# Wider spacing of the cosine chains, goals per period for the weight conversion, and earlier y rows in a fused attention and two-layer feed-forward kernel

## The chip, the cores and the metric

The kernel runs on one core of one Trainium2 chip. The metric is the device time of one execution in microseconds. PE is TensorE's matrix engine, PEld its weight loads, DVE is VectorE, ACT is ScalarE, POOL is GpSimd, and SP is SyncE, which here issues nearly all DMAs.

## The reference, cut to what matters

```python
def reference(q, k, v, omega, moe_*, moe2_*):
    q_p, k_p = phi(q * scale), phi(k * scale)      # random features: exp of a projection
    x = (q_p @ (k_p.T @ v)) / (q_p @ k_p.sum(0) + 1e-06)     # per head; 4 x 8 heads, 576 rows
    x = x.transpose(0, 2, 1, 3).reshape(2304, 512)
    xn = x / sqrt(mean(x * x) + 1e-06) * rms_g
    x = (silu(xn @ w_gate) * (xn @ w_val)) @ w_out          # layer 1: 512 -> 1536 -> 512
    h = x @ moe2_w_in                                       # layer 2: 512 -> 2048 -> 512
    return (h * cos(h)) @ moe2_w_out
```

The large weights of both layers arrive as float64, that is as pairs of 32-bit words; the kernel computes in float32.

## The kernel before

Every matrix product of the two layers is made of three passes over float32 values that are split into a high and a low part, so a weight has to be turned into such a pair before PE can use it. Class `Weights` does this in two halves. A **front** takes one chunk (128x512) from two 32-bit words to one float32: ACT scales the exponent (L182), DVE works on the bits (L190, L193 for some chunks, L195, L204) and POOL adds the low part (L209); the result is stored to DRAM (`keep`, L347). A **back** fetches it again, on every second chunk makes sums and differences on DVE (L274, L287, L289, L291), and splits it (ACT L214, POOL L217) into a buffer of a ring of 20. Neither has a place of its own: `pace(front, back)` adds two rates to two credits and runs as many steps as the credits allow, so these steps go into each engine's queue wherever `pace` is called. `rate(chunks, steps)` says how many front steps a call must run for `chunks` chunks to be done after `steps` calls. A back whose chunk isn't kept yet, or that finds no free buffer, is put off.

The program has four stages: attention (to 96 us), layer 1's first part (96 to 301 us), where attention's last rows, four columns of hidden units and the weights share a step, layer 1's second and third part (301 to 590 us) and layer 2. From 301 us on the products are made in pairs of blocks with seven multiplications in place of eight (functions `duo`, `ys`, `hidden`).

Layer 2 runs in 24 **periods** (k = 0 to 23). A period has seven products `hidden(k, i)`, i = 0 to 6, each of six matmuls into one of two PSUM banks, Xh or Yh, by turns. A product adds to what the bank's last one left, so PE can't begin product i + 2 before the bank has been read for product i: for i = 0, 2, 3, 6 by an ACT copy (L1190), for i = 1, 4, 5 by a DVE addition (L1193). Twice in a period, after products 1 and 5, `cosine` starts a **chain** on two rows of features: ACT counts the turns (Identity), DVE takes them off (two operations, `reduce`), ACT takes the sine, DVE multiplies (L1225), ACT and DVE split the result (`cut`, L1046 and L1049). Between the products PE gets `share[i]` matmuls of the output products `out2` (36 to a period, L1242), which run about a period behind because they need the chains' results. `out2` ends a run of periods on the same blocks in periods 4, 7, 13, 16, 21 and 23 (`ends_run` two periods before): its six sums are then taken out of PSUM by `evict` (L1267, L1274, L1276), and the next run begins in the same banks.

What comes when is told by a clock of **units**: `at(d, f)` puts `f` off by d units, and `unit()` runs what is due, then `pace(*tempo)`, which is the front and back rate of the period. There are two units to a product, so 14 to a period. Each engine then works its queue strictly in the order in which the code issued it.

`ask` (in `after_second`) fetches a y row from DRAM `later` units after a product; `add_y` (L1099) adds it to layer 1's sum; `mix` makes from the sums the combinations that layer 2 reads.

Of the kernel before, what the change touches and what calls it, by code (L numbers as in the profile page):

```python
# [38 lines left out]
AF = mybir.ActivationFunctionType  # L39
ALU = mybir.AluOpType  # L40
# [16 lines left out]
def attention_then_ffn(ctx: ExitStack, tc: tile.TileContext, qT, kT, v, omT, wc1, rms_g, wc2, out, B, H, S, D):  # L57
    nc = tc.nc
# [486 lines left out]
    with tc.manual_schedule():  # L545
# [402 lines left out]
        for n, (g, blk, f, first, last) in enumerate(steps):  # L948
            tail = n >= N1 - G
            if tail:  # L950
                wts.freed = C1 * f
            back = 2.0 if tail else wts.rate_back(C1 * G + 5, N1 - G - n) / 2
            if wts.n_front < 6 * FRONT:
                back = 0.0
            rates = wts.rate(FRONTS_BY_1, N1 - G + 1 - n) / 2 if n <= N1 - G else 0.0, back
            if n < G:
                rates = max(rates[0], 4), rates[1]
            s = SLOTS + 2 * n
            load_ahead(s)
            older(s, -7, -5)  # L960
            ps = product(blk, f, 0)
            a = silu(blk, f, ps)
            older(s, -6, -4, -3, -2, -1)
            begin(s)
            if n >= 1:
                out1(*steps[n - 1][:3], hid[n - 1], *steps[n - 1][3:], (0, 1))
            older(s, 1, 0)
            job(2 if tail else 3)
            wts.pace(*rates)
            job(0 if tail else 3)  # L970
            if n > N1 - G and early_names:
                bring(1, 0, early_names.pop(0))
            flush(3)
            load_ahead(s + 1)
            older(s + 1, -7, -5)
            ps = product(blk, f, 1)
            hid[n] = gated(blk, f, a, ps)
            older(s + 1, -6, -4, -3, -2, -1)
            begin(s + 1)
            if n >= 1:  # L980
                out1(*steps[n - 1][:3], hid.pop(n - 1), *steps[n - 1][3:], (2, 3))
            older(s + 1, 1, 0)
            job(2 if tail else 3)
            wts.pace(*rates)
            job(0 if tail else 3)
            flush(3)
            if n == N1 - G:
                assert s + 2 > max(then)
                while len(combined) < 2:
                    job(1)  # L990
                combine.close()
                open_between()
                limit[0] = NPAIR
                tp[:] = [combine.enter_context(tc.tile_pool(name="combinations2", bufs=3, reuse_waits="tile")), 3]
                early_names = ["B11", "B21", "T2", "T1", "T4"]
            if n >= N1 - G and early_names:
                bring(1, 0, early_names.pop(0))
# [206 lines left out]
        def cosine(k, h, of, begin=1):  # L1204

            name = "_".join(f"{x}_{f}_{blk}" for x, f, blk in of)
            span = slice(0, 2) if len(of) == 2 else slice(begin, begin + 1)
            h = h[:, span]
            a = two_rows(I32, f"turns{name}")[:, span]
            b = f32(halves(f"r{name}"))[:, span]  # L1210
            r = f32(a)

            def reduce():
                nc.vector.scalar_tensor_tensor(b, a, -TWO_PI_HI, h, op0=ALU.mult, op1=ALU.add)  # L1214
                nc.vector.scalar_tensor_tensor(r, a, -TWO_PI_LO, b, op0=ALU.mult, op1=ALU.add)  # L1215

            def cut(i):
                o = turned[of[i]] = halves("o%d_%d_%d" % of[i])
                split(o, r[:, i])
                at(int(of[i][0] + 1 < NPER), lower, o, r[:, i], nc.vector)  # L1220

            at(1, nc.scalar.activation, a, h, AF.Identity, quarter, 1.0 / (2 * math.pi))
            at(2, reduce)
            at(3, nc.scalar.activation, r, r, AF.Sin, half_pi)
            at(4, lambda: nc.vector.tensor_tensor(r, h, r, op=ALU.mult))  # L1225
            for i in range(len(of)):
                at(5 + i, cut, i)

        def out2(k):

# [57 lines left out]
        for k, (g, p) in enumerate(pairs):  # L1288
# [10 lines left out]
                made["y"] = 0  # L1299
            front[0] = wts.rate(FRONTS_BY_2, left) if left > 0 else 0.0  # L1300
            tt = {}
            later = 3 if g == 1 else 9

            def after_first(i, f):
                if k == 0 and i == 0 and f == fs[1]:
# [25 lines left out]
                wts.freed = start + PER_GROUP  # L1331
            if g == 2:
                for m, (name, kk) in enumerate((name, kk) for kk in range(2) for name in ("T1", "T3", "T2", "T4")):
                    at(6 + 3 * m // 2 if p else 6 + (0, 2, 3, 6)[m % 4] + 14 * kk, mix, p, name, kk)

        def stream():
            for k in range(NPER):
# [2 lines left out]
        def freed_by(k):  # L1340
# [4 lines left out]
            elif sessions[n - 1][0] != g and fq == GROUPS2[g][0]:  # L1345
                wts.freed = first_tile[g]

        o = stream()
        for k in range(1, NPER):
            loading = ends_run[k]  # L1350
            tempo[:] = 0.0 if loading or k < 4 else wts.rate(len(wts.todo) + 1, 14 * (14 - k)), 0.5 if loading else 1.3
            if ends_run[k - 1]:
                ask_sums(k - 1)
            share = [2, 3, 3, 4, 4, 5, 5] if k == 1 else [5, 5, 3, 5, 6, 6, 6] if begins_run[k - 1] else [5, 5, 5, 5, 5, 5, 6]
            for i in range(7):
                if (k, i) == (len(GROUPS2[0]), 4):
                    assert not whole
# [5 lines left out]
                for _ in range(share[i]):  # L1363
                    next(o)
                unit()
                if i == 1 and k > 1:
                    freed_by(k - 1)
                if (i, k + 1) == (3, NPER):
                    ask_sums(k)
# [53 lines left out]
```

## Time and profile before

| what | us |
|---|---|
| time, median of 3 (from, to) | 992.25 (991.57, 992.88) |
| profiled execution: time | 990.3 |
| profiled execution: span | 988.5 |
| PE busy (share of the span) | 957.0 (97%) |
| DVE busy | 730.0 (74%) |
| ACT busy | 532.0 (54%) |
| POOL busy | 412.1 (42%) |

The rows of the trace stand below, in numbered groups. A table of windows gives, for each stretch of time, its length, then the busy time of PE, PEld, DVE, ACT and POOL with the number of instructions, the granted clock, the DMA engines' share and GB/s. In a timeline a row has its start and length in us; what stands in brackets is how long the engine was idle before and whose result ended that. The periods of layer 2 are told apart by the start of their first product.

### The profile page before, as it was taken

What the parts mean: (1) busy time and instruction counts of PE and PEld (TensorE: products, weight loads), DVE (VectorE), ACT (ScalarE), POOL (GpSimd) and SP (SyncE); (2) the same over time, 40 slices, a digit from 0 to 9 for tenths busy, and PEclk for the clock granted to TensorE, in tenths of its full rate; (3) what the DMA queues carried; (4) which work ended last, traced back from release to release, by engine and by line L of the source; (5) the groups of instructions that cost most, each with busy time, mean ns of one, the idle gap of its engine ahead of it and who ended that gap; (6) DMA issues with size and microseconds to landing.
All of it is one profiled execution on the core that took longest, in us unless ns stands there. A gap on an engine that the chain in (4) does not pass through costs nothing.

```text
span 988.5 us, 16243 instructions
## 1 busy us (share of the span) xinstructions
PE 957.0 (97%) x5761; PEld 895.3 (91%) x5761; DVE 730.0 (74%) x1175; ACT 532.0 (54%) x1143; POOL 412.1 (42%) x377
## 2 busy tenths in 40 slices
PE   9999999998999999999999997999988999999998
PEld 8998999998999999999999996989867879898987
DVE  6787678898854785576786659887898897776766
ACT  7787676676434442535353636554554645464443
POOL 3143348648926875455664743211334121040000
PEclk9999999999999999999999999999999999999999
DMA  8555268876796988766979793857533848306564
GB/s 310 156 175 173 85 226 281 275 286 213 268 334 235 393 279 319 246 191 216 345 270 389 255 343 103 308 187 239 181 127 113 282 139 300 115 22 225 203 253 150
DMA packets 96082, 227.65 MB, mean 230 GB/s; under 512 B 9728, under 2 KB 45184, under 8 KB 96000
## 3 DMA queue, kind: packets, MB, share of 16 engines
q1 hardware_dynamic: 94560, 221.81, 64.8%
q10 hardware_dynamic: 1440, 4.78, 1.4%
q8 instruction: 46, 0.75, 0.3%
q14 instruction: 36, 0.29, 0.1%
HBM read 156.04 MB, written 70.52 MB: 229 GB/s over the span
## 4 chain that ended last, share of the span: by engine, by line
PE 61%; DVE 13%; DMA 8%; issue 6%; POOL 5%; ACT 5%; SPq 1%; ACTq 0%; DVEq 0%; POOLq 0%
PE o_ps L1242 14%; PE Xh L1038 7%; PE gv_ps L831 6%; PE X L1038 6%; PE Yh L1038 5%; PE Y L1038 4%; PE kv_ps L587 4%; PE y L1144 4%; PE y_ps L884 3%; DMA y<-y_dram 3%; PE num_ps L464 2%; PE kp_ps L426 2%; DMA T<-T_dram 1%; DVE r L1214 1%; PE qp_ps L426 1%
## 5 line engine op out<-in xcount | busy, mean ns | idle before, releaser
L1242 PE MATMUL o_ps<-w,o 128*128 128x512 f32 x864 | 225.7, 393 | 1.0 <-DVE o L1274 0.8
L209 POOL TENSOR_TENSOR f<-f,raw 128x512 f32<-128x512 f32 x68 | 94.5, 1390 | 225.2 <-DVE raw L204 193.3
L217 POOL TENSOR_TENSOR w<-b,w 128x512 fp32r<-128x512 f32 x88 | 116.1, 1325 | 169.7 <-ACT w L214 147.0
L1242 PEld LDWEIGHTS o_ps<-w,o 128*128 128x128 f32 x864 | 159.6, 188 | 25.7 <-DVE o L1274 1.1
L831 PE MATMUL gv_ps<-xhl,w 128*128 128x384 f32 x576 | 109.8, 339 | 1.5 <-DVE eT L454 1.3
L1144 PE MATMUL y<-t,w 128*128 128x384 f32 x576 | 102.7, 335 | 1.8 <-POOL w L217 1.8
L831 PEld LDWEIGHTS gv_ps<-xhl,w 128*128 128x128 f32 x576 | 101.8, 190 | 2.6 <-DVE eT L454 2.0
L1144 PEld LDWEIGHTS y<-t,w 128*128 128x128 f32 x576 | 99.9, 188 | 2.8 <-POOL w L217 2.8
L1038 PE MATMUL Xh<-T,w 128*128 128x384 f32 x432 | 88.9, 340 | 5.3 <-ACT h L1190 5.3
L1038 PEld LDWEIGHTS Xh<-T,w 128*128 128x128 f32 x432 | 77.8, 188 | 13.6 <-ACT h L1190 8.2
L1012 ACT ACTIVATE turns<-turns,half_pi 128x768 f32<-128x768 f32 (+1 forms) x50 | 45.6, 913 | 76.7 <-DVE turns L1215 76.7
L1038 PE MATMUL X<-T,w 128*128 128x384 f32 x432 | 81.1, 335 | 0.5 <-POOL w L217 0.3
L1038 PEld LDWEIGHTS X<-T,w 128*128 128x128 f32 x432 | 75.3, 188 | 1.1 <-POOL w L217 0.7
L1012 ACT ACTIVATE turns<-h,quarter 128x768 int32<-128x768 f32 (+1 forms) x50 | 45.6, 912 | 56.6 <-DVE h L1193 56.5
L1225 DVE TENSOR_TENSOR turns<-h,turns 128x768 f32<-128x768 f32 (+1 forms) x50 | 50.6, 1012 | 31.3 <-ACT turns L1012 31.1
L214 ACT CAST w<-b 128x512 fp32r<-128x512 f32 x88 | 50.7, 581 | 30.7 <-DVE b L274 28.2
L1049 DVE TENSOR_TENSOR o<-turns,o 128x384 fp32r<-128x384 f32 x96 | 64.8, 704 | 2.5 <-ACT o L1046 1.3
L1038 PE MATMUL Yh<-B,w 128*128 128x384 f32 x288 | 59.3, 340 | 7.1 <-ACT h L1190 5.7
L1214 DVE SCALAR_TENSOR_TENSOR r<-turns,h 128x768 f32<-128x768 int32 (+1 forms) x50 | 50.2, 1004 | 21.2 <-ACT turns L1012 20.8
L1038 PEld LDWEIGHTS Yh<-B,w 128*128 128x128 f32 x288 | 51.7, 188 | 13.0 <-ACT h L1190 8.0
L884 PE MATMUL y_ps<-t,w 128*128 128x384 f32 x288 | 60.7, 346 | 0.0
L1046 ACT CAST o<-turns 128x384 fp32r<-128x384 f32 x96 | 45.8, 512 | 25.5 <-DVE turns L1225 24.4
(118 smaller groups left out, 1863.9 us busy)
## 6 DMA issues: line engine op xcount, KB each, us to landing
T<-T_dram SPq DMA_DIRECT2D x48, 768.0 KB, 7.0
raw<-wc SPq DMA_DIRECT2D x59, 512.0 KB, 5.0
B<-yh_dram SPq DMA_DIRECT2D x21, 768.0 KB, 5.3
kept<-f SPq DMA_DIRECT2D x56, 256.0 KB, 5.1
b<-kept SPq DMA_DIRECT2D x56, 256.0 KB, 4.6
B<-x_dram SPq DMA_DIRECT2D x15, 768.0 KB, 6.4
x_dram<-xhl SPq DMA_DIRECT2D x12, 768.0 KB, 5.8
s<-x_dram SPq DMA_DIRECT2D x24, 384.0 KB, 6.1
```

The costliest lines, as they stand in the source:

```text
L209: nc.gpsimd.tensor_tensor(f32(f), f32(f), rest, op=ALU.add)
L214: nc.scalar.copy(t[:, 0, to], src)
L217: nc.gpsimd.tensor_tensor(t[:, 1, to], src, f32(t[:, 0, to]), op=ALU.subtract)
L831: nc.tensor.matmul(o, w[i], x[j], start=n == 0, stop=n == len(terms) - 1)
L884: nc.tensor.matmul(yacc[blk][e], w[:, i, e * P:(e + 1) * P], t[:, j], start=first and i + j == 0, stop=last and j == 1)
L1012: f(*args)
L1038: nc.tensor.matmul(o, w[:, i, c + kk * P:c + (kk + 1) * P], x[:, j, kk], start=begin and n == 0, stop=n == 5, skip_group_check=True)
L1049: engine.tensor_tensor(t[:, 1], a, f32(t[:, 0]), op=ALU.subtract)
L1144: nc.tensor.matmul(acc[e], w[:, i, e * P:(e + 1) * P], t[:, j], start=f == fs[0] and i + j == 0, stop=f == fs[-1] and j == 1)
L1214: nc.vector.scalar_tensor_tensor(b, a, -TWO_PI_HI, h, op0=ALU.mult, op1=ALU.add)
L1225: at(4, lambda: nc.vector.tensor_tensor(r, h, r, op=ALU.mult))
L1242: nc.tensor.matmul(oacc[blk][j], o[:, x, js], w[:, y], start=first and n == 0, stop=last and n == 2)
```

## The change

Lines after line 965 move down by 2 to 6, so L1193 of before is L1197 of the changed kernel, L1225 is L1230, L1049 is L1053, L1242 is L1247 and L1274 is L1279.

```diff
             begin(s)
+            if n >= G:
+                wts.pace(rates[0], 0.0)
             if n >= 1:
                 out1(...)
             older(s, 1, 0)
             job(2 if tail else 3)
-            wts.pace(*rates)
+            wts.pace(rates[0] if n < G else 0.0, rates[1])
...
-            at(1, nc.scalar.activation, a, h, AF.Identity, quarter, 1.0 / (2 * math.pi))
-            at(2, reduce)
-            at(3, nc.scalar.activation, r, r, AF.Sin, half_pi)
-            at(4, lambda: nc.vector.tensor_tensor(r, h, r, op=ALU.mult))
+            ph, re, si, mu, cu = (1, 2, 3, 4, 5) if k + 1 == NPER else (1, 3, 5, 6, 7)
+            at(ph, nc.scalar.activation, a, h, AF.Identity, quarter, 1.0 / (2 * math.pi))
+            at(re, reduce)
+            at(si, nc.scalar.activation, r, r, AF.Sin, half_pi)
+            at(mu, lambda: nc.vector.tensor_tensor(r, h, r, op=ALU.mult))
             for i in range(len(of)):
-                at(5 + i, cut, i)
+                at(cu + i, cut, i)
...
-            later = 3 if g == 1 else 9
+            later = 3 if g == 1 else 7
...
-                    at(6 + 3 * m // 2 if p else 6 + (0, 2, 3, 6)[m % 4] + 14 * kk, mix, p, name, kk)
+                    at(6 + 5 * m // 4 if p else 6 + (0, 2, 3, 6)[m % 4] + 14 * kk, mix, p, name, kk)
...
+        FRONT_GOALS = {3: 42, 4: 45, 6: 47, 7: 48, 8: 49, 9: 50, 12: 52, 13: 54, 15: 56, 16: 57}
...
-            tempo[:] = 0.0 if loading or k < 4 else wts.rate(len(wts.todo) + 1, 14 * (14 - k)), 0.5 if loading else 1.3
+            tempo[:] = wts.rate(wts.fused + FRONT_GOALS[k], 14) if k in FRONT_GOALS else 0.0, 0.5 if loading else 1.3
...
-            share = [2, 3, 3, 4, 4, 5, 5] if k == 1 else [5, 5, 3, 5, 6, 6, 6] if begins_run[k - 1] else [5, 5, 5, 5, 5, 5, 6]
+            share = [1, 2, 3, 3, 4, 4, 4] if k == 1 else [5, 5, 3, 5, 6, 6, 6] if begins_run[k - 1] else [5, 5, 5, 5, 5, 5, 6]
...
-                if i == 1 and k > 1:
+                if i == 2 and k > 1:
                     freed_by(k - 1)
```

In words, part by part. In **layer 1's first part**, from the fifth step on, a step's front work is issued before the output products of the step before, and its back work where both stood. On PE, ACT and DVE this leaves the order of that stage as it was; on POOL four front additions and three combinations change places with neighbours, and on SP some twenty fetches and stores change places with a neighbour.

The **chains** (all but the last period's) get two units more: one between the turns and `reduce`, one between `reduce` and the sine. As their results come later, period 1 gets 21 output matmuls for 26, so that from there on `out2` stands five matmuls further back, to the end.

The **fronts** of layer 2 no longer run at one rate from period 4 to 13, but to a goal for each of ten periods. The order of DVE's queue gives these numbers of front rows (L190, L195 and L204 together) and back rows (L274, L287, L289 and L291 together) in each period:

| period | 3 | 4 | 5 | 6 | 7 | 8 | 9 | 10 | 11 | 12 | 13 | 14 | 15 | 16 |
|---|---|---|---|---|---|---|---|---|---|---|---|---|---|---|
| front rows before | 0 | 4 | 1 | 5 | 6 | 6 | 6 | 6 | 2 | 5 | 8 | 2 | 0 | 0 |
| front rows now | 5 | 8 | 3 | 4 | 6 | 3 | 3 | 1 | 0 | 4 | 6 | 2 | 4 | 2 |
| back rows before | 0 | 0 | 3 | 1 | 0 | 1 | 3 | 4 | 0 | 0 | 4 | 0 | 0 | 0 |
| back rows now | 0 | 4 | 0 | 0 | 0 | 0 | 4 | 4 | 0 | 0 | 1 | 3 | 0 | 0 |

The **y rows** of layer 1's third part are asked for two units earlier, and two of the three pairs of blocks start their combinations a little closer together.

*First place:* ACT's queue where period 1 goes over into period 2. `h6_1<-Xh_1` and `h6_1<-Xh_2` are the copies that free Xh after product 6 of period 1 and product 0 of period 2; the row with `half_pi` is the sine of the chain `turns1_3_5_1_2_5`. Before:

```order
L1012 ACTIVATE turns1_3_5_1_2_5_7118<-h2_1_7053,quarter_74 128x768
L1190 COPY h6_1_7142<-Xh_1_7000 128x384
L1012 ACTIVATE turns1_3_5_1_2_5_7118<-turns1_3_5_1_2_5_7118,half_pi_75 128x768
L214 CAST w64_7158<-b47_7032 128x512
L1190 COPY h6_1_7142<-Xh_2_7160 128x384
```

Now:

```order
L1194 COPY h6_1_7138<-Xh_1_6998 128x384
L214 CAST w64_7152<-b47_7028 128x512
L1194 COPY h6_1_7138<-Xh_2_7154 128x384
L1127 CAST T4h0_0_7164<-y2_0_2_6740 128x384
L1016 ACTIVATE turns1_3_5_1_2_5_7111<-turns1_3_5_1_2_5_7111,half_pi_75 128x768
L1050 CAST o1_3_5_7192<-turns1_3_5_1_2_5_7111 128x384
L1016 ACTIVATE turns1_3_4_2_4_4_7182<-h6_1_7138,quarter_74 128x768
L1194 COPY h2_2_7205<-Xh_2_7154 128x384
```

The sine moved from ahead of the copy of product 0 to behind it.

*Second place:* DVE's queue in period 9 and at the start of 10. `h2_9<-Xh_9`, `h2_9<-Yh_9` and `h6_9<-Yh_10` are the additions that free the banks after products 4 and 5 of period 9 and product 1 of period 10; rows of `raw` and `f` are fronts. Before:

```order
L1193 TENSOR_TENSOR h2_9_8273<-Xh_9_8223,h2_9_8273 128x384
L1049 TENSOR_TENSOR o8_5_0_8309<-turns8_5_0_9_6_0_8250,o8_5_0_8309 128x384
L1049 TENSOR_TENSOR o9_6_0_8320<-turns8_5_0_9_6_0_8250,o9_6_0_8320 128x384
L190 TENSOR_SCALAR f60_8333<-W60_8299 128x512
L1193 TENSOR_TENSOR h2_9_8273<-Yh_9_8222,h2_9_8273 128x384
L195 TENSOR_SCALAR raw60_8196<-f60_8333 128x512
L1214 SCALAR_TENSOR_TENSOR r9_7_1_9_6_1_8343<-turns9_7_1_9_6_1_8342,h2_9_8273 128x768
L1215 SCALAR_TENSOR_TENSOR turns9_7_1_9_6_1_8342<-turns9_7_1_9_6_1_8342,r9_7_1_9_6_1_8343 128x768
L204 SCALAR_TENSOR_TENSOR raw60_8196<-raw60_8196 128x512
L1225 TENSOR_TENSOR turns9_7_1_9_6_1_8342<-h2_9_8273,turns9_7_1_9_6_1_8342 128x768
L1193 TENSOR_TENSOR h6_9_8359<-Yh_10_8381,h6_9_8359 128x384
```

Now:

```order
L1197 TENSOR_TENSOR h2_9_8283<-Xh_9_8238,h2_9_8283 128x384
L1230 TENSOR_TENSOR turns8_5_0_9_6_0_8261<-h6_8_8223,turns8_5_0_9_6_0_8261 128x768
L195 TENSOR_SCALAR raw61_8034<-f61_8288 128x512
L1197 TENSOR_TENSOR h2_9_8283<-Yh_9_8237,h2_9_8283 128x384
L1053 TENSOR_TENSOR o8_5_0_8334<-turns8_5_0_9_6_0_8261,o8_5_0_8334 128x384
L1053 TENSOR_TENSOR o9_6_0_8349<-turns8_5_0_9_6_0_8261,o9_6_0_8349 128x384
L1218 SCALAR_TENSOR_TENSOR r9_7_1_9_6_1_8348<-turns9_7_1_9_6_1_8347,h2_9_8283 128x768
L1219 SCALAR_TENSOR_TENSOR turns9_7_1_9_6_1_8347<-turns9_7_1_9_6_1_8347,r9_7_1_9_6_1_8348 128x768
L204 SCALAR_TENSOR_TENSOR raw61_8034<-raw61_8034 128x512
L1197 TENSOR_TENSOR h6_9_8367<-Yh_10_8386,h6_9_8367 128x384
```

The multiplication of a chain (second row, `turns8_5_0_9_6_0`) now comes between the additions of products 4 and 5, and that of the chain begun here comes after the addition of the next period's product 1 (it isn't among these rows any more); of four front rows in the piece two are left.

*Third place:* the hand-over of the output banks in period 4, first on PE. `o_ps0_4_2` is the third bank of the run that ends, `o_ps3_2_2` takes the same bank for the run that begins. Before:

```order
L1242 MATMUL o_ps0_4_2_7012<-w64_7158,o2_5_4_7390 128x512 x3
L1038 MATMUL Xh_4_7450<-T2_3_1_7225,w56_6847 128x384 x6
L1242 MATMUL o_ps3_2_0_7517<-w52_6617,o3_0_2_7403 128x512 x3
L1038 MATMUL Yh_4_7451<-T1_3_1_7243,w55_6784 128x384 x6
L1242 MATMUL o_ps3_2_1_7518<-w52_6617,o3_0_2_7403 128x512 x3
L1242 MATMUL o_ps3_2_2_7519<-w52_6617,o3_0_2_7403 128x512 x2
```

Now:

```order
L1247 MATMUL o_ps0_4_2_7011<-w64_7152,o2_5_4_7419 128x512
L1042 MATMUL Yh_4_7475<-T1_3_1_7235,w55_6786 128x384 x6
L1247 MATMUL o_ps0_4_2_7011<-w64_7152,o2_5_4_7419 128x512 x2
L1247 MATMUL o_ps3_2_0_7565<-w52_6624,o3_0_2_7430 128x512 x3
L1042 MATMUL Xh_4_7474<-T3_3_1_7258,w56_6847 128x384 x6
L1247 MATMUL o_ps3_2_1_7566<-w52_6624,o3_0_2_7430 128x512 x3
L1247 MATMUL o_ps3_2_2_7567<-w52_6624,o3_0_2_7430 128x512 x3
```

Between the last matmul of the old sum and the first of the new in that bank there stood two products and six output matmuls, now one product and six.

The same place in DVE's queue, from just behind the addition of product 1 of period 4 to that of product 4; `L1274` and `L1279` are evictions. Before:

```order
L1049 TENSOR_TENSOR o3_1_3_7465<-turns3_1_3_3_0_3_7419,o3_1_3_7465 128x384
L1049 TENSOR_TENSOR o3_0_3_7486<-turns3_1_3_3_0_3_7419,o3_0_3_7486 128x384
L1274 COPY o2_4_2_7501<-o_ps0_4_2_7012 128x512
L195 TENSOR_SCALAR raw51_6318<-f51_7475 128x512
L1214 SCALAR_TENSOR_TENSOR r3_1_2_4_2_2_7485<-turns3_1_2_4_2_2_7484,h6_3_7433 128x768
L1215 SCALAR_TENSOR_TENSOR turns3_1_2_4_2_2_7484<-turns3_1_2_4_2_2_7484,r3_1_2_4_2_2_7485 128x768
L1225 TENSOR_TENSOR turns3_1_2_4_2_2_7484<-h6_3_7433,turns3_1_2_4_2_2_7484 128x768
L204 SCALAR_TENSOR_TENSOR raw51_6318<-raw51_6318 128x512
L1193 TENSOR_TENSOR h2_4_7513<-Xh_4_7450,h2_4_7513 128x384
```

Now:

```order
L1230 TENSOR_TENSOR turns3_1_3_3_0_3_7428<-h2_3_7364,turns3_1_3_3_0_3_7428 128x768
L204 SCALAR_TENSOR_TENSOR raw53_7345<-raw53_7345 128x512
L190 TENSOR_SCALAR f54_7512<-W54_7506 128x512
L1279 COPY o2_5_2_7525<-o_ps0_5_2_7094 128x512
L1279 COPY o2_4_0_7528<-o_ps0_4_0_7009 128x512
L1053 TENSOR_TENSOR o3_1_3_7521<-turns3_1_3_3_0_3_7428,o3_1_3_7521 128x384
L195 TENSOR_SCALAR raw54_7400<-f54_7512 128x512
L1218 SCALAR_TENSOR_TENSOR r3_1_2_4_2_2_7504<-turns3_1_2_4_2_2_7503,h6_3_7452 128x768
L1219 SCALAR_TENSOR_TENSOR turns3_1_2_4_2_2_7503<-turns3_1_2_4_2_2_7503,r3_1_2_4_2_2_7504 128x768
L1053 TENSOR_TENSOR o3_0_3_7539<-turns3_1_3_3_0_3_7428,o3_0_3_7539 128x384
L1279 COPY o2_4_2_7573<-o_ps0_4_2_7011 128x512
L1197 TENSOR_TENSOR h2_4_7537<-Xh_4_7474,h2_4_7537 128x384
```

Two more evictions, the multiplication of another chain and a row of a front (`f54`) came into this stretch, and the eviction of the third bank (`o2_4_2`) moved from its start to its end.

## Rows read from the trace of the kernel before

**Rows 1.** PE's waits from 590 us on: who waited for whom, us in total, times, longest
```profile
PE Yh L1038 <- ACT h L1190: 5.7, 5, 2.4
PE Xh L1038 <- ACT h L1190: 5.3, 6, 2.2
PE Xh L1038 <- DVE h L1193: 2.8, 3, 1.2
...
PE o_ps L1242 <- DVE o L1274: 0.8, 1, 0.8
```

**Rows 2.** Periods of layer 2: window, its length, then each engine's busy us, clock, DMA.
```profile
593.40:610.60 17.20, 14.48 (x71) 11.71 (x69) 15.52 (x27) 11.14 (x22) 5.29 (x3) 1.00 0.22 78
610.60:628.90 18.30, 16.07 (x79) 14.18 (x79) 17.63 (x24) 10.56 (x20) 6.80 (x7) 1.00 0.80 287
628.90:644.70 15.80, 15.80 (x80) 14.22 (x79) 12.80 (x16) 7.08 (x12) 3.97 (x3) 1.00 0.56 220
644.70:660.40 15.70, 15.70 (x80) 14.13 (x79) 13.49 (x23) 9.39 (x16) 1.31 (x1) 1.00 0.58 200
...
707.60:726.00 18.40, 16.47 (x80) 13.85 (x78) 16.21 (x20) 9.29 (x18) 7.26 (x5) 1.00 0.39 127
726.00:746.10 20.10, 16.55 (x79) 13.94 (x79) 18.63 (x23) 10.00 (x19) 8.98 (x7) 1.00 0.42 129
746.10:766.00 19.90, 16.82 (x79) 13.86 (x79) 17.13 (x24) 10.49 (x20) 8.94 (x7) 1.00 0.38 112
766.00:782.30 16.30, 16.07 (x79) 14.16 (x80) 13.25 (x16) 9.99 (x17) 4.42 (x4) 1.00 0.87 302
798.00:816.80 18.80, 16.64 (x79) 13.89 (x79) 17.92 (x30) 10.22 (x18) 6.04 (x4) 1.00 0.41 140
832.60:848.30 15.70, 15.70 (x79) 14.18 (x78) 9.23 (x14) 7.41 (x12) 0.00 (x0) 1.00 0.51 181
```

**Rows 3.** Timeline of 612.5 to 618 us: start, length, operation, idle before.
```profile
614.64 0.96 DVE L1215 SCALAR_TENSOR_TENSOR turns<-turns,r 128x768 f32<-128x768 int32 x1
...
615.63 0.94 ACT L1012 ACTIVATE turns<-turns,half_pi 128x768 f32<-128x768 f32 x1 [3.70 <-DVE turns L1215]
...
617.50 0.79 PE L1038 MATMUL Xh<-T,w 128*128 128x384 f32 x3 [2.23 <-ACT h L1190]
```

**Rows 4.** PE's timeline from 832.6 us on, where nothing waits.
```profile
832.59 1.21 PE L1038 MATMUL Xh<-B,w 128*128 128x384 f32 x6
833.63 1.31 PE L1242 MATMUL o_ps<-w,o 128*128 128x512 f32 x5
834.79 1.23 PE L1038 MATMUL Yh<-B,w 128*128 128x384 f32 x6
```

**Rows 5.** DVE's groups of 832.6 to 848.3 us: busy, mean ns of one, idle before.
```profile
L1049 DVE TENSOR_TENSOR o<-turns,o 128x384 fp32r<-128x384 f32 x4 | 2.0, 550 | 0.0
```

**Rows 6.** DVE's groups of 726.0 to 746.1 us, the longest period.
```profile
L1049 DVE TENSOR_TENSOR o<-turns,o 128x384 fp32r<-128x384 f32 x4 | 4.7, 1188 | 0.0
...
L190 DVE TENSOR_SCALAR f<-W 128x512 int32<-128x512 int32 x2 | 1.9, 974 | 0.0
...
L204 DVE SCALAR_TENSOR_TENSOR raw<-raw 128x512 f32<-128x512 uint32 x2 | 1.4, 684 | 0.0
L195 DVE TENSOR_SCALAR raw<-f 128x512 int32<-128x512 int32 x3 | 1.2, 415 | 0.0
...
L289 DVE TENSOR_TENSOR b<-b 128x256 f32<-128x256 f32 x1 | 0.4, 417 | 0.0
```

**Rows 7.** DVE's groups of 691.9 to 707.6 us, the same operation unhindered.
```profile
L190 DVE TENSOR_SCALAR f<-W 128x512 int32<-128x512 int32 x2 | 0.8, 412 | 0.0
```

**Rows 8.** Waits of the whole run: the three that the other edits touch.
```profile
DVE y L1099 <- DMA y<-y_dram: 16.6, 9, 4.4
...
PE qp_ps L426 <- DVE xhl L516: 2.6, 1, 2.6
...
PE Yh L1038 <- DVE y L1099: 1.4, 1, 1.4
```

More of the change, by code (lines that the diff above doesn't have):

```diff
@@ L979, in attention_then_ffn @@
             begin(s + 1)
+            if n >= G:
+                wts.pace(rates[0], 0.0)
             if n >= 1:
@@ L983, in attention_then_ffn @@
             job(2 if tail else 3)
-            wts.pace(*rates)
+            wts.pace(rates[0] if n < G else 0.0, rates[1])
             job(0 if tail else 3)
```

## The prediction

> **What bounds the kernel now.** I read the table of windows first, then PE's waits, then the timeline around a wait. In a period of layer 2 in which nothing else happens PE works from end to end: 15.7 us, with DVE busy for only 9.23 [rows 2]. That is the least a period can take, since PE's work is the same in each. PE's timeline there gives its parts: a product takes 1.04 us from its start to the next (833.63 - 832.59), five output matmuls 1.16 (834.79 - 833.63), so 0.23 each [rows 4]. Seven products and 36 output matmuls make 15.7.
>
> So every microsecond over 15.7 in a period is one that PE lost. [Rows 2] show where: periods 8, 9, 10 and 11 took 18.4, 20.1, 19.9 and 16.3, in sum 74.7 for 62.8, **11.9 lost**; period 13 18.8, **3.1 lost**; period 2 18.3, 2.6 lost; period 1 17.2, but with only 26 output matmuls its least is 15.7 - 10 x 0.23 = 13.4, so 3.8 lost: **6.4** for the two. That is 21.4 us in layer 2. PE's waits name the culprit: the copies of ACT and the additions of DVE that free Xh and Yh [rows 1]. The four rows sum to 14.6, less than 21.4; shorter gaps and slower restarts make the rest.
>
> Why are they late? Two things come together. First, DVE has too much to do: in the five costly periods 8, 9, 10, 13 and 2 it was busy for 16.2, 18.6, 17.1, 17.9 and 17.6 us [rows 2], all above 15.7. Second, what PE needs stands behind something that itself waits: at 615.63 ACT's sine had waited 3.70 us for DVE's `reduce`, which ended at 615.60 (614.64 + 0.96), with the copy that frees Xh queued behind it, and PE began 2.23 us late [rows 3].
>
> **The fronts, periods 8 to 11.** DVE's queue there loses 4 rows L190, 4 L195 and 3 L204 in periods 8 to 10 (18 front rows to 7), and two more in period 11; the back rows stay. In the longest period these rows took 0.97, 0.42 and 0.68 us [rows 6], L190 0.41 where nothing disturbed it [rows 7]. That is 4 x 0.41 (or 0.97) + 4 x 0.42 + 3 x 0.68 = 5.4 to 7.6 us of the 16.2 + 18.6 + 17.1 = 51.9 that DVE was busy. Left are 44.3 to 46.5, against 3 x 15.7 = 47.1. So DVE fits, but barely, and period 9, which keeps its backs, may still be a little over. I leave 1.0 us lost of the 11.9: **-10.9**. The bounds: all 11.9, or half of it if POOL and not DVE's count is what matters (below).
>
> **Period 13** loses two front rows and three back rows: 0.41 + 0.68 + 3 x 0.42 = 2.35 of 17.9 [rows 2, 6, 7], which leaves 15.6 for 15.7. I leave 0.7 of 3.1 lost: **-2.4** (0 to -3.1).
>
> **The wider chains.** In the first place shown of ACT's queue the sine now stands behind the copy that it held up, and `reduce` has a unit more before the sine is due. DVE has no less work by this. It matters most in periods 1 and 2, whose DVE work is otherwise nearly unchanged and where PE lost 6.4. DVE was busy for 15.5 and 17.6 us of 35.5 [rows 2], so at most 2.4 of the 6.4 were idle time of DVE that a better order can win, and I give it **-1.5** (-2.4 to +1.2). The upper end: period 1 gives five output matmuls (5 x 0.23 = 1.2) to the end of the kernel, and if DVE sets the end of period 2 alone, that is a loss. The last tail is longer by these five, which is in the same 1.2.
>
> **Where the fronts go.** Period 3 gets 2 L190, 2 L195, 1 L204: 0.8 + 0.8 + 0.7 = 2.3, so 12.8 becomes 15.1 [rows 2]. Period 4 gets one L190, one L195, two L204 and four back rows more: 0.4 + 0.4 + 1.4 + 1.7 = 3.9, so 13.5 becomes 17.4, 1.7 over, with no slack in period 3 before it. The trace has a period of this very make-up, 13 of before (8 front rows, 4 back rows, 4 evictions on DVE): 3.1 lost. Period 5 is light again, so some of the queue can run over into it. I take **+1.8** (0 to 3.1). Periods 12, 14, 15 and 16 get at most 4 front rows each, 2.2 us over a quiet 9.2 (13.3 or so with period 16's six sums); that has cover, zero. If it failed, period 16 would be first.
>
> **The hand-over of the output banks.** In periods 4, 7, 13, 16, 21 and 23 the third bank was taken again 2 x 1.04 + 6 x 0.23 = 3.5 us after its last matmul, now 1.04 + 6 x 0.23 = 2.4 [rows 4]. In this time DVE must reach the eviction and do it. Before, PE waited for it once, 0.8 us [rows 1]. In quiet periods 2.4 is enough. Period 4 is counted above; for period 7 with its six front rows I take **+0.4** (0 to 1.2).
>
> **y rows two units earlier.** DVE waited nine times for y rows, 16.6 us in all, and PE once behind that, 1.4 us [rows 8]. Two units are over 2 us: **-1.2** (0 to -1.4). Closer combinations on POOL: zero.
>
> **Layer 1's first part.** PE's, ACT's and DVE's queues hold the same rows in the same order. The stage's one large wait, 2.6 us behind DVE's `xhl` [rows 8], stays. Zero; as only POOL and SP move, between -2.6 and +2.6.
>
> **The sum:** -10.9 - 2.4 - 1.5 + 1.8 + 0.4 - 1.2 = -13.8. It is made against the profiled execution: 990.3 - 13.8 = 976.5. The median of the three runs, 992.25, lies 1.95 above that execution, so for a median I forecast **978.5**. With each term at its own end but not all at once, 974 to 985.
>
> **Rival 1, POOL sets DVE's pace.** DVE's splits took 550 ns each in a quiet period with POOL idle [rows 5] and 1188 in period 9 [rows 6], with POOL busy for 9.0 us [rows 2]; DVE was busy there 18.6 - 9.2 = 9.4 us more than in the quiet period, while its six front rows and three back rows (6 x 0.69 + 3 x 0.42 = 5.4, from the averages of 0.97, 0.42 and 0.68 there) explain little over half. So some 4 us of a busy period come from POOL's presence. The moved fronts leave POOL's back additions in periods 8 to 10, and take their own additions on POOL to periods 3 and 4. Then the first term is half, -6; period 13 -1.2; and period 4 costs not 1.7 but 1.7 + 4 = 5.7. In sum -6 - 1.2 - 1.5 + 5.7 + 0.4 - 1.2 = -3.8: 988.5. Against it: POOL's three additions of the removed fronts leave periods 8 to 10 with them. The Trainium skill has a rule for this (SBUF — State Buffer, section Who interferes with whom): an operation of VectorE with two inputs in SBUF and one of GpSimd that reads SBUF can't overlap, one of them waits for all of the other. By that rule the rival would hold in full and its time be 988.5; the trace agrees as far as 550 and 1188 go, though even there the splits took double and not a whole POOL operation more each.
>
> **Rival 2, all of layer 2's waits go.** The added slack takes up period 4 as well and frees periods 1 and 2: -11.9 - 3.1 - 3.6 - 1.2 = -19.8: 972.5. For it: ACT and DVE idle in waits for each other in every period. Against it: DVE's 17.4 in period 4.
>
> **Rival 3, slower: the third bank.** At each of the six hand-overs PE reaches the old bank 1.1 us sooner than before, while DVE's eviction of it moved back behind two more evictions and a multiplication (the last place shown). If DVE is more than the 2.4 us behind there, less the eviction itself, PE stops for the rest, and what waits on PE stops too. At the price of the worst period that lost to an eviction, 3.1, six make 18.6, and with 0.4 of it counted already 978.5 + 18.2 = 996.7. Against it: in periods 16, 21 and 23 DVE has few rows but sums.
>
> **Rival 4, it doesn't matter:** the waits only move from periods 8 to 13 to 3 to 5 and 12 to 16, since all 51 front rows are still done; 992.
>
> **How the numbers follow.** The forecast 0.60, rival 1 0.15, rival 2 0.12, rival 3 0.08, rival 4 0.05. The range for eight in ten takes the forecast's 974 to 985, half of rival 1 above it and nearly all of rival 2 below: 971 to 988. What can be told from no change by a measurement here is about 0.2%, 2 us. Faster by more than that: 0.60 + 0.12 + 0.15 = 0.87; within it 0.05; slower 0.08.
>
> **What would show it.** In the table of windows by periods, 8 to 10 should each be 15.7 to 16.5 with DVE at 14 to 16.5 us, 13 at most 16.5, and period 4 between 16 and 18.5, with PE's wait there on an addition or the third bank. A first part 2 us shorter or longer would say that POOL's order counted. If periods 8 to 10 stay above 17.5 though they have 11 front rows less, the first term is wrong, and rival 1 right.

## The result, and the profile after

The changed kernel takes 978.81 us (median of 4 runs, 978.06 to 979.79) for 991.91 of the kernel before on the same chip: a ratio of 0.9867, interval 0.985 to 0.9884. The profiled execution took 978.17, its span 976.4, where before had 990.3 and 988.5: 12.1 us less by the profiles, 13.1 by the medians.

The periods of layer 2 in the table of windows of the changed kernel (length, then busy time of PE, PEld, DVE, ACT and POOL with counts, clock, DMA) answer to [rows 2]: period 0, then 1 to 4, then 8 to 11, 13 and 16. The last row of [rows 2] is period 15; periods 0 and 16 of the kernel before stand below the table.

```profile
578.40:592.00 13.60, 13.60 (x80) 13.60 (x80) 8.62 (x16) 7.16 (x15) 4.40 (x4) 1.00 1.03 390
...
592.00:606.80 14.80, 12.88 (x64) 10.86 (x63) 14.73 (x24) 9.28 (x19) 5.25 (x3) 1.00 0.20 71
606.80:625.10 18.30, 16.66 (x79) 14.05 (x80) 17.77 (x23) 11.79 (x22) 6.85 (x6) 1.00 0.74 255
625.10:641.50 16.40, 15.93 (x79) 14.07 (x78) 15.94 (x23) 7.54 (x13) 5.95 (x4) 1.00 0.93 361
641.50:660.10 18.60, 16.29 (x79) 13.97 (x79) 18.31 (x30) 11.11 (x21) 5.37 (x4) 1.00 0.51 170
...
707.30:723.10 15.80, 15.80 (x80) 14.22 (x79) 12.77 (x16) 9.31 (x17) 6.70 (x5) 1.00 0.27 90
723.10:738.80 15.70, 15.70 (x79) 14.04 (x78) 14.87 (x18) 8.16 (x17) 8.33 (x6) 1.00 0.33 102
738.80:754.60 15.80, 15.80 (x79) 14.26 (x79) 14.39 (x20) 10.86 (x20) 6.21 (x5) 1.00 0.05 17
754.60:770.40 15.80, 15.80 (x80) 14.22 (x79) 13.19 (x16) 8.03 (x14) 5.31 (x3) 1.00 0.83 280
786.10:801.80 15.70, 15.70 (x79) 14.14 (x78) 13.46 (x22) 9.11 (x16) 4.92 (x4) 1.00 0.61 202
...
833.40:849.90 16.50, 15.93 (x79) 14.08 (x78) 14.05 (x21) 7.53 (x13) 3.38 (x3) 1.00 0.50 176
```

Before, period 0 and period 16:

```profile
578.10:593.40 15.30, 13.87 (x79) 13.41 (x79) 8.97 (x14) 5.68 (x12) 3.44 (x4) 1.00 0.90 312
...
848.30:864.10 15.80, 15.80 (x80) 14.18 (x79) 13.33 (x20) 7.77 (x14) 1.14 (x1) 1.00 0.51 168
```

Periods 8 to 11 are now at the least a period can take, 63.1 us for 74.7, and so is 13, 15.7 for 18.8. Period 0 takes 13.6 for 15.3 and waits for nothing. What came in its place stands in periods 3 and 4 (16.4 and 18.6 for 15.8 and 15.7) and 16 (16.5 for 15.8).

PE's waits from 578 us on, which answer to [rows 1] (who waited for whom, us in total, times, longest):

```profile
PE Yh L1042 <- DVE h L1197: 2.3, 2, 1.2
PE Xh L1042 <- ACT h L1194: 1.5, 3, 0.7
PE o_ps L1247 <- DVE o L1279: 1.2, 1, 1.2
PE o_ps L1247 <- DVE o L1053: 1.2, 1, 1.2
PE o_ps L1247 <- DVE sum L1272: 0.9, 2, 0.6
```

The waits for ACT's copies, 11.0 us in [rows 1], are down to 1.5. Two kinds are new or larger: for evictions (`o` L1279, `sum` L1272), and once, in period 1, for the split of a chain's result (`o` L1053), which the wider spacing made later: the kernel with the chains alone, below, waits there just as long.

And one of PE's waits in the whole run, which answers to [rows 8]:

```profile
PE qp_ps L426 <- DVE xhl L516: 2.2, 1, 2.2
```

The first part's large wait shrank from 2.6 to 2.2 us, but a wait for `eT` (L454) at 160 us grew from 0.3 to 1.0. That is a draw.

### The profile page after: what moved, and what is told of

It reads as the page before. It is cut to its first block, busy times and chain, and to the rows that moved or that the text cites. A ratio compares the mean times of both kernels' runs of the same rounds, so it can differ in the third digit from the quotient of the medians.

```text
span 976.4 us, 16226 instructions
## 1 busy us (share of the span) xinstructions
PE 955.3 (98%) x5761; PEld 896.5 (92%) x5761; DVE 724.2 (74%) x1175; ACT 531.4 (54%) x1143; POOL 420.2 (43%) x377
## 5 line engine op out<-in xcount | busy, mean ns | idle before, releaser
L1247 PE MATMUL o_ps<-w,o 128*128 128x512 f32 x864 | 226.3, 393 | 3.3 <-DVE o L1279 1.2
L1247 PEld LDWEIGHTS o_ps<-w,o 128*128 128x128 f32 x864 | 159.4, 188 | 28.9 <-DVE sum L1272 1.8
L217 POOL TENSOR_TENSOR w<-b,w 128x512 fp32r<-128x512 f32 x88 | 119.5, 1366 | 125.9 <-ACT w L214 116.6
L1050 ACT CAST o<-turns 128x384 fp32r<-128x384 f32 x96 | 47.2, 512 | 81.6 <-DVE turns L1230 81.6
L1053 DVE TENSOR_TENSOR o<-turns,o 128x384 fp32r<-128x384 f32 x96 | 61.8, 659 | 8.5 <-ACT o L1050 8.1
L214 ACT CAST w<-b 128x512 fp32r<-128x512 f32 x88 | 50.5, 581 | 31.7 <-DVE b L274 26.0
L204 DVE SCALAR_TENSOR_TENSOR raw<-raw 128x512 f32<-128x512 uint32 x68 | 55.3, 813 | 0.6
L1219 DVE SCALAR_TENSOR_TENSOR turns<-turns,r 128x768 f32<-128x768 int32 (+1 forms) x50 | 54.3, 1086 | 1.7
L1197 DVE TENSOR_TENSOR h<-Yh,h 128x384 f32<-128x384 f32 x48 | 26.6, 553 | 38.3 <-PE Yh L1042 38.3
```

Of the source, the lines that this page charges most:

```text
L204: nc.vector.scalar_tensor_tensor(rest, raw[:, :, 0].bitcast(U32), 2.0 ** -52, rest, op0=ALU.mult, op1=ALU.mult)
L214: nc.scalar.copy(t[:, 0, to], src)
L217: nc.gpsimd.tensor_tensor(t[:, 1, to], src, f32(t[:, 0, to]), op=ALU.subtract)
L1050: nc.scalar.copy(t[:, 0], a)
L1053: engine.tensor_tensor(t[:, 1], a, f32(t[:, 0]), op=ALU.subtract)
L1247: nc.tensor.matmul(oacc[blk][j], o[:, x, js], w[:, y], start=first and n == 0, stop=last and n == 2)
```

## The experiments

My theory: the microseconds of DVE's front rows overfill periods 8 to 13, so the goals win them and the wider chains help a little in periods 1 and 2. The rivals: the chains' stalls are the cause, or POOL's additions, which hold DVE up.

**Goals and chains apart.** The first kernel has the goals alone, the second the chains alone, the third both without the rest.

```diff
# e1: the kernel before, and
+        FRONT_GOALS = {3: 42, 4: 45, 6: 47, 7: 48, 8: 49, 9: 50, 12: 52, 13: 54, 15: 56, 16: 57}
+            tempo[:] = wts.rate(wts.fused + FRONT_GOALS[k], 14) if k in FRONT_GOALS else 0.0, ...
# e2: the kernel before, and
+            ph, re, si, mu, cu = (1, 2, 3, 4, 5) if k + 1 == NPER else (1, 3, 5, 6, 7)
+            share = [1, 2, 3, 3, 4, 4, 4] if k == 1 else ...
+                if i == 2 and k > 1:
# e3: both
```

> The kernel before with the front goals alone; chains, y rows and layer 1's first part as before. Theory (DVE's front rows are what overfills periods 8 to 13): periods 8, 9, 10 and 13 fall to 15.7 to 16.5 us with narrow chains too, period 4 grows to 17.5 to 19, so about 11 of the 13 us are won: 980 to 982. Rival (the narrow chains' stalls are the cause, the fronts only load them): periods 8 to 10 stay above 17.5 and no more than 4 us are won: 988 or more. Rival (POOL's share of the port): half, about 986.

> The kernel before with the wider chains alone (and what belongs to them: 21 output matmuls in period 1, buffers freed a product later); fronts at one rate from period 4 to 13. Theory (DVE's rows): periods 9 and 10 stay at 18.5 us or more, 13 too, and 1 to 3 us are won in all, mostly in periods 1 and 2: 989 to 991. Rival (chains): periods 8 to 13 fall to 16.5 or less and 8 us or more are won: 984 or less.

> Goals and chains together, without the y rows' two units, without the closer combinations and without layer 1's first part. Theory (the parts add up): 12.5 us of 13 won, 979 to 981, and period 0 at 15 us as before. If the rest of the change carries more than 2.5 us: above 981.5.

| kernel | median, us | ratio to before (interval) | periods 8 to 11 | 13 | 3 to 5 | 1 and 2 |
|---|---|---|---|---|---|---|
| before | 991.58 | | 74.7 | 18.8 | 47.2 | 35.5 |
| goals alone | 988.57 | 0.9972 (0.996 to 0.9984) | 67.3 | 15.7 | 50.8 | 37.1 |
| chains alone | 983.58 | 0.9916 (0.9891 to 0.994) | 68.8 | 16.9 | 47.2 | 33.1 |
| both | 981.41 | 0.9907 (0.9874 to 0.994) | 63.0 | 15.7 | 50.8 | 33.1 |

The lengths are from the first product of one period to that of the next in the profiled execution. Periods 8 to 10 of the first, in whose layer 2 the clock fell twice (a mean of 0.91 in period 2, 0.92 in period 9), then those of the second:

```profile
713.90:729.60 15.70, 15.70 (x79) 14.18 (x78) 13.27 (x16) 8.47 (x16) 6.76 (x5) 1.00 0.25 86
729.60:749.70 20.10, 17.89 (x80) 15.27 (x79) 16.62 (x21) 10.64 (x20) 7.69 (x6) 0.92 0.34 93
749.70:765.40 15.70, 15.70 (x79) 14.19 (x78) 11.98 (x18) 9.46 (x17) 6.42 (x5) 1.00 0.00 0
```

```profile
705.90:721.60 15.70, 15.70 (x79) 14.19 (x78) 13.98 (x18) 8.02 (x15) 7.82 (x5) 1.00 0.54 174
721.60:740.50 18.90, 16.71 (x79) 13.70 (x77) 18.08 (x23) 10.59 (x19) 10.93 (x7) 1.00 0.33 107
740.50:758.90 18.40, 16.57 (x79) 13.97 (x79) 17.23 (x24) 10.60 (x19) 8.50 (x7) 1.00 0.37 108
```

My split fell, and neither case held as it was written. The goals alone won 3 us, not 10 to 12, though of periods 8, 9, 10 and 13 only period 9 stayed long; the chains alone won 8, not 1 to 3, though periods 9 and 10 stayed at 18.9 and 18.4. In periods 8 to 11 the goals take 7.4 of the 11.9 lost. The fall of the clock in period 9 cost (1 - 0.92) x 20.1 = 1.6 us, so it is about 9.0 at the full clock. The chains take 5.9, and only both take all. The goals alone also made periods 7 and 14 longer, 17.1 and 17.4 us for 15.7 and 15.8, each with a wait of PE for a copy of ACT (1.1 and 1.4 us). With the chains added, both are back at 15.7 and 15.8: this, the 3.6 us of periods 3 to 5 and the clock are why the goals alone won so little. Goals and chains together won 10.2 us by the medians, less than the 12.5 expected; in that run's period 0, 17.3 us long, PE waited 2.0 us for a y row, and the clock's mean was 0.90.

With the goals alone PE still waited 2.1 us in period 9 for a copy of ACT, in a period in which DVE was busy for 16.6 of 20.1 us: that is not a full queue. With the chains alone DVE had the same work in all, was busy for 49.3 us in periods 8 to 10 instead of 51.9 (two operations fewer fell into them), and the three took 53.0 instead of 58.4. The engines' waits for each other in layer 2 show what changed. Before, ACT's sine waited 76.7 us for `reduce`, its turns 56.5 for an addition and its split 24.4 for the multiplication, each with what is behind it in ACT's queue, the copies that PE needs among it; and DVE waited for ACT:

```profile
ACT turns L1012 <- DVE turns L1215: 76.7, 49, 3.9
ACT turns L1012 <- DVE h L1193: 56.5, 32, 3.4
ACT o L1046 <- DVE turns L1225: 24.4, 33, 1.6
```

```profile
DVE turns L1225 <- ACT turns L1012: 31.1, 41, 1.0
DVE r L1214 <- ACT turns L1012: 20.8, 23, 1.1
```

and with the chains alone:

```profile
ACT o L1046 <- DVE turns L1226: 85.4, 47, 2.9
...
ACT turns L1012 <- DVE turns L1215: 32.4, 30, 3.0
ACT turns L1012 <- DVE h L1193: 7.7, 12, 1.4
```

```profile
DVE r L1214 <- ACT turns L1012: 3.8, 12, 0.7
DVE turns L1226 <- ACT turns L1012: 2.2, 5, 0.7
```

ACT's three waits fell only from 157.6 to 125.5 us in sum, since most of the waiting moved to the split. What fell is what others felt of it. DVE's two waits for ACT went from 51.9 to 6.0 us, and in periods 8 to 10, where DVE had little time to give away, from 5.4 to 0.7. PE's waits for ACT's copies in these three periods went from 5.7 to 0.9, while those for DVE's additions stayed (2.8, then 3.0).

**DVE's rows or POOL's additions.** Both kernels are the kernel before with one operation of layer 2's 17 fronts left out: POOL's addition in the first, one of DVE's three rows in the second.

```diff
# e4
+            if c < 51:
                 nc.gpsimd.tensor_tensor(f32(f), f32(f), rest, op=ALU.add)
# e5
+            if c < 51:
                 nc.vector.scalar_tensor_tensor(rest, raw[:, :, 0].bitcast(U32), 2.0 ** -52, rest, ...)
```

> The kernel before, with POOL's addition of the low part (1.3 us each) left out of the 17 fronts of layer 2, so that those weights are rounded; DVE's rows are all there. Theory (DVE's and ACT's queues and their waits for each other set periods 8 to 13): at most 2 us won, 989.5 to 991.5, periods 9 and 10 still above 18.5. Rival (POOL's use of the port it shares with DVE stretches DVE's rows): periods 8, 9 and 10 fall by 1.5 us or more each, 985 to 987.

> The kernel before, with DVE's row L204 (0.68 us each) left out of the 17 fronts of layer 2, so that their low part is wrong; POOL's additions are all there. It is the counterpart of the kernel without POOL's additions, which won 7.0 us, 6.7 of them in periods 8 to 11. Theory 1 (a microsecond of DVE's queue costs the same whether it is a row or a row held up by POOL): 2 rows a period, 1.4 us less in each of periods 8, 9, 10 and 13, 4 to 6 us won, 986 to 988. Theory 2 (only POOL's hold on the port counts): less than 2 us, 990 or more.

Without POOL's additions: 985.13 us, ratio 0.993 (0.9913 to 0.9947), 7.0 us less, as the rival of the first expectation had it, except that period 10 fell by 1.1 us only. Without DVE's row: 989.92, 0.9972 (0.9962 to 0.9983), 2.6 us less. Periods 8 to 11 took 68.0 and 72.9 us for 74.7. So the seven POOL additions in them, whose results DVE doesn't wait for, cost 6.7 us, and seven of DVE's own rows, 4.8 us of its queue, 1.8. DVE's busy time in periods 8 to 10 tells by which way: without POOL's additions it fell from 51.9 to 45.3 us, with all of DVE's rows still there (66 operations in the three windows, before 67). In period 13 it was the other way round: 18.6 us without the additions, 17.5 without DVE's row, for 18.8. Period 9 of the kernel without POOL's additions, window and DVE's group L190, which had taken 974 ns there [rows 6]:

```profile
725.10:742.10 17.00, 15.97 (x80) 14.07 (x79) 16.27 (x22) 9.04 (x18) 6.46 (x5) 1.00 0.40 115
```

```profile
L190 DVE TENSOR_SCALAR f<-W 128x512 int32<-128x512 int32 x2 | 0.8, 416 | 0.0
```

Of the second expectation's two theories, the second (only POOL's hold counts) is nearer, though its "less than 2" was passed by a little, and period 13 speaks for the first. In periods 8 to 11 a front costs more through its POOL addition than through this one of its three rows on DVE; the other two rows weren't tried. This is in the way that the rule on the shared pair of ports in the Trainium skill (SBUF — State Buffer, section Who interferes with whom) has it: one operation waits for all of the other. The trace agrees in the timelines under the next heading: a `reduce` that began at 653.50, beside a POOL addition of 653.19 to 654.75, ended at 655.57, 0.8 us after it, and takes 0.95 us elsewhere.

**Period 4.** Two kernels take something out of the head or the tail of the new busy period.

```diff
# e7: the changed kernel, and
-        FRONT_GOALS = {3: 42, 4: 45, 6: 47, 7: 48, 8: 49, 9: 50, ...}
+        FRONT_GOALS = {3: 42, 4: 43, 5: 44, 6: 46, 7: 47, 8: 49, 9: 50, ...}
# e10: the changed kernel, and in tempo
-  0.5 if loading else 1.3
+  0.0 if k == 4 else 0.5 if loading else 1.3
```

> The changed kernel with other goals: period 4 gets 5 front rows on DVE for 8, periods 5, 6, 8 and 9 one or two more each, 7 two fewer. Theory (the 8 front rows with 4 evictions and 4 back rows overfill period 4, the others have room): period 4 falls from 18.6 to 16.5 to 17.5, periods 5 to 10 stay below 16, 977 to 978. Rival (a row costs the same wherever it goes): 978.8, with 8 and 9 above 16.

> The changed kernel with the back rate 0 in period 4, which moves three of its four back rows on DVE (0.42 us each, ahead of the addition that frees Yh after product 1) and a POOL subtraction to period 5; the 8 front rows stay. Theory (that pile at the head of period 4, and not the number of front rows, makes PE wait 1.1 us for the addition and 1.2 for the eviction): period 4 falls from 18.6 to 17.4 or less, 977 to 977.8. Rival (period 4 has too much in all): 18.2 or more, 978.8.

Fewer fronts in period 4: 980.75 us, 0.988 (0.9866 to 0.9895). That is no gain, and by the profiles a loss: period 4 took 19.0 us with 5 front rows where it took 18.6 with 8, and period 9 17.2 where it took 15.7. Which rows meet counts as well as how many there are: in this kernel a POOL addition began just ahead of a chain's `reduce`, which took 2.07 us instead of the 0.95 it has otherwise (timeline; start, length):

```profile
653.19 1.56 POOL L209 TENSOR_TENSOR f<-f,raw 128x512 f32<-128x512 f32 x1 [6.09 <-DVE raw L204]
...
653.50 2.07 DVE L1218 SCALAR_TENSOR_TENSOR r<-turns,h 128x768 f32<-128x768 int32 x1
```

The timeline of the changed kernel shows what the first wait of period 4 was about. The addition that frees Yh (L1197 at 648.40) stood behind an eviction, a front row and three back rows, after `reduce` had taken 1.93 us beside a POOL subtraction that began at 644.31. Ahead of that a front row (L190 at 641.77) had taken 1.48 us instead of 0.42, beside a POOL addition that began at 641.66. The last row is PE's, with its wait of 1.1 us:

```profile
644.48 1.93 DVE L1219 SCALAR_TENSOR_TENSOR turns<-turns,r 128x768 f32<-128x768 int32 x1
646.34 0.68 DVE L1279 COPY o<-o_ps 128x512 f32<-128x512 f32 x1
646.94 0.41 DVE L195 TENSOR_SCALAR raw<-f 128x512 int32<-128x512 int32 x1
647.27 0.41 DVE L287 TENSOR_TENSOR b<-b,b 128x256 f32<-128x256 f32 x1
647.72 0.42 DVE L289 TENSOR_TENSOR b<-b 128x256 f32<-128x256 f32 x1
648.06 0.42 DVE L291 TENSOR_TENSOR b<-b,b 128x256 f32<-128x256 f32 x1
648.40 0.55 DVE L1197 TENSOR_TENSOR h<-Yh,h 128x384 f32<-128x384 f32 x1
649.00 1.33 PE L1042 MATMUL Yh<-T,w 128*128 128x384 f32 x6 [1.11 <-DVE h L1197]
```

With the backs off in that period: 976.9 us, 0.9847 (0.9834 to 0.986). Period 4 falls by 1.1 us, to 17.5, with all 8 front rows still in it:

```profile
640.70:658.20 17.50, 16.30 (x80) 14.04 (x79) 17.23 (x27) 10.63 (x20) 5.36 (x4) 1.00 0.54 182
```

That is half of the theory, which had 17.4 or less: PE's wait of 1.1 us for the addition is gone, but that of 1.2 for the eviction is still there. The trace shows also that only the three back rows left the period; the POOL subtraction stayed, and `reduce` still took 1.93 us beside it. Period 5, which has the back rows now, took 15.7.

**The hand-over of the banks.** A later short share gives the third bank its 3.5 us again; then together with the lighter period 4, in both forms.

```diff
# e6 the changed kernel, e8 with e7's goals, e11 with e10's back rate, and
-  [5, 5, 3, 5, 6, 6, 6] if begins_run[k - 1]
+  [5, 5, 5, 3, 6, 6, 6] if begins_run[k - 1]
```

> The changed kernel with the short share of 3 output matmuls one product later in the periods that follow the start of a run, so that the third bank's old sum ends before a product and not in the middle of a share: 3.5 us from its last matmul to the bank's next, as before the change. Theory (the hand-over's shorter time causes PE's waits on evictions, 1.2 us in period 4, 0.6 in 16, 0.3 in 23): these waits go, 1.5 to 2 us less than the changed kernel, 977. Rival (DVE is late anyway and PE then waits at the next product's bank instead): 978.8.

> Both edits of the two kernels before this one, the later short share and the lighter period 4. Theory: the gains add up, periods 4 at 16 or less, 16 and 23 at 15.8 and without waits on evictions: 975 to 976.5. Rival: no more than either alone, 977 or more.

> The same with the later short share as well (which won 0.7 us by its median, within the noise, and 0.5 us in period 16). Theory: the two add up, as the hand-over's wait is the shorter the less stands ahead of the eviction: 976 to 977. Rival: no better than either alone, 977.5 to 978.5.

The share alone: 978.09 us, 0.9857 (0.9837 to 0.9877), which can't be told from the changed kernel. With fewer fronts in period 4: 980.04, 0.9874 (0.9859 to 0.9889), where the gains were expected to add up to 976.5 or less; the lighter period 4 had none to add. With the backs off: **976.82**, 0.9842 (0.9828 to 0.9855), the fastest here by its median, but within the noise of the kernel with the backs off alone, so that it doesn't show that the two add up. The traces show more than the times. Of the share alone, periods 4 and 16:

```profile
640.60:659.20 18.60, 16.22 (x79) 13.98 (x78) 18.29 (x30) 11.09 (x21) 5.37 (x4) 1.00 0.51 170
832.70:848.70 16.00, 15.97 (x80) 14.10 (x79) 13.53 (x21) 7.42 (x13) 3.41 (x3) 1.00 0.52 182
```

In period 16, where DVE has little more than its sums, the longer time won back 0.5 us. In period 4 it won nothing, since DVE is late there whatever PE does in between: PE's wait for the addition fell from 1.1 to 0.7 us, and that on the eviction grew from 1.2 to 1.7.

**The y rows and the first part.** Each is undone alone in the changed kernel.

```diff
# e9
-            later = 3 if g == 1 else 7
+            later = 3 if g == 1 else 9
# e12
-                wts.pace(rates[0], 0.0)
-            wts.pace(rates[0] if n < G else 0.0, rates[1])
+            wts.pace(*rates)
```

> The changed kernel with the y rows asked for nine units after the product again. Theory: PE's wait of 1.4 us in period 0 comes back, period 0 takes 15 us for 13.6, so 1.2 to 1.7 us more than the changed kernel's 978.8: 980 to 980.5. If the closer combinations removed it: 978.8.

> The changed kernel with layer 1's first part as before (fronts and backs at one place). Theory (only POOL and SP move there, PE's waits change from 0.3, 0.2 and 2.6 us to 1.0, 0 and 2.2 us): no difference, 978.3 to 979.3. Rival (the part is worth the 0.9 us that the goals and chains together and the y rows leave unexplained): 979.7 or more.

With the y rows late: 980.54 us, 0.9886 (0.986 to 0.9912) for the changed kernel's 0.9867, 1.7 us more by the medians. The intervals overlap, but period 0 shows it, 16.3 us for 13.6, even more than the 15 expected:

```profile
577.10:593.40 16.30, 14.12 (x81) 13.48 (x80) 10.02 (x16) 6.76 (x14) 3.81 (x4) 1.00 0.90 312
```

With the first part as before: 977.47 us, 0.9849 (0.9835 to 0.9862). So this part of the change is worth nothing, or costs a microsecond or two (1.3 by the medians); the intervals overlap, and PE's waits in the stage differ by 0.2 us in sum.

## Why the prediction came out as it did

The forecast of 978.5 us was met, within 0.3, and part of that is luck. The sum was made against the profiled execution and gave 976.5 us for it; it took 978.17, 1.7 more. The median was then to lie 1.95 us above that execution, and lies 0.6 above it (978.81 - 978.17), 1.3 less. These two misses cancel. Within the sum, too, terms that were too small cancel with others that were too large, and the largest had the right size for a reason that was half wrong. What the prediction had named as its signs came out so: periods 8 to 10 at 15.7 and 15.8, 13 at 15.7, and period 4 at 18.6, a little over the 18.5 named, with PE waiting there for an addition and for the third bank.

- **Periods 8 to 11, -10.9:** measured -11.6. The place and the size were right. The step that failed is the one that gave all of it to the fronts and reckoned with DVE's microseconds. DVE was left with 42.0 us in periods 8 to 10, less than the 44.3 to 46.5 reckoned. But with the goals alone it was busy for only 41.9 us there, and period 9 still took 20.1. The goals alone win 7.4 there, about 9.0 at the full clock, and the chains alone 5.9. Of a front, leaving out the POOL addition wins 6.7 there, one of the three DVE rows 1.8.
- **Period 13, -2.4:** -3.1. Goals alone -3.1, chains alone -1.9.
- **The wider chains, -1.5, in periods 1 and 2:** there 33.1 us for 35.5, so -2.4, and the last stretch, from period 23's first product to the end, 31.7 for 30.0: -0.7 in all, within the range. The sentence "DVE has no less work by this" was true, but the conclusion was not. The idle time of DVE, as the most that a better order can win, was reckoned for periods 1 and 2 alone, where the same reckoning for 8 to 10 ([rows 2]: 58.4 us long, 51.9 busy) would have given up to 6.5. With the chains alone these three won 5.4, of which 2.8 was idle time of DVE and 2.6 busy time that went; period 11 won 0.5 more. This is the term that was mis-sized: by the medians the chains are worth 8.0 us by themselves, by the two profiles 6.2 (982.3 for 988.5).
- **Where the fronts go, +1.8:** +3.6 in periods 3 to 5, the upper bound and a little more (0 to 3.1). The period of the same make-up, 13 of before, had been the right row to look at, and 3.1 the better value, as no slack stood ahead. The eight front rows, which the term was named after, were not all of it: three back rows moved out win 1.1 us, three front rows, put at other steps, none. Of the 1.8 us that are still lost there, PE waits 1.2 for the eviction; how much of that the front rows make isn't shown.
- **The hand-over, +0.4 in period 7:** nothing in 7, 0.7 in period 16, of which the later share wins back 0.5. So 2.4 us were not enough in this quiet period; the chains alone, which bring the shorter time but no front rows to it, have 16.5 us there too.
- **y rows, -1.2:** -1.7 in period 0 of the two profiles, a little past the range's -1.4; 2.7 against the changed kernel with them late.
- **The first part, 0:** measured 0 within what can be told.

By the profiles -11.6 - 3.1 - 0.7 + 3.6 + 0.7 - 1.7 = -12.8, for a span that fell by 12.1. Of the rivals, the third (the third bank at six hand-overs) failed by its price: in two of the six PE waits for more than half a microsecond (1.2 and 0.6). The first (POOL sets DVE's pace) was right in its mechanism in periods 8 to 10, by the kernel without POOL's additions, and wrong in what follows from it: period 4 cost 2.9 us, not 5.7, and periods 8 to 10 lost all but one of their POOL additions with the fronts, which was said against it. None of my cases held that goals and chains each win a good part by themselves, and that the goals without the chains lose some of it again in periods 7 and 14.

What stays open: how much of the POOL addition's cost is its hold on DVE and how much that POOL is free earlier for its other work, since it was left out whole; why DVE's row counts for more than POOL's addition in period 13; why two front rows at other steps made period 9 of the kernel with the lighter period 4 longer by 1.5 us (its POOL was busy for 9.0 us there instead of 8.3, which may be it), and whether the closer combinations do anything; they weren't tried alone.

## What to carry to other kernels

Where engines that work their queues in order pass a chain of small steps to and fro, put a step into a queue only when its input will be there: a step that waits holds up everything behind it, and here two units more between the steps won more than half of the whole change by themselves. Before costing a moved operation by its own length, look for what it makes the other engine wait: in periods 8 to 11 here an addition of 1.3 us on POOL did more harm than 0.7 us in DVE's own queue, though not in period 13. And when periods are over their limit, add up the idle time of the busy engine in each of them: it is a first measure of what a better order can win there without moving any work (6.5 us here, for 5.4 won).

## What the hardware showed that I had not expected

TensorE's granted clock falls now and then, at places that change from run to run: of the profiled executions two show no fall (the changed kernel with the later short share, and with the y rows late), that of the goals alone shows three, goals and chains together two, the others one place each. A mean of 0.89 over 15 us tells that the clock stood at the lower of its two levels, 1.2 GHz, for a part of them, which cost 0.11 x 15 = 1.6 us of PE's work at the full clock. The kernel before had its fall in the first window, 90 to 105 us, the changed kernel in the second, 225 to 240 us; the other window is at 1.00 in each:

```profile
90.00:105.00 15.00, 13.87 (x86) 13.21 (x86) 9.35 (x18) 10.85 (x21) 6.12 (x6) 0.89 0.22 71
```

```profile
225.00:240.00 15.00, 12.78 (x82) 12.03 (x81) 11.56 (x21) 9.66 (x23) 11.69 (x13) 0.89 0.58 184
```

The same two waits of PE stand ahead of both places in both kernels, 1.0 us at 97 and 2.2 to 2.6 at 231, and the clock fell after the one in the first run and after the other in the second. The profiled run of the kernel with the goals alone had falls after waits of 2.2 and 2.1 us in periods 2 and 9 as well, and that with goals and chains after one of 2.0 us in period 0. So it seems that a wait of PE of one or two microseconds is now and then paid for a second time; no run takes out one wait to test it.

This bears on the medians. The 41 executions of the kernel before that were taken beside the experiments had a mean granted clock of 0.993 to 0.998: the nine at 0.998 took 990.5 us on average, the eighteen at 0.995 or less 992.9. The four of the changed kernel all had 0.998, the four of the chains alone 0.998 to 1.000. So a microsecond or two of the 13.1, and of the chains' 8.0, may be falls of the clock that didn't happen; the profiles of the kernel before, of the changed one and of the chains alone, with one fall each, differ by 12.1 and 6.2 us.
